# Gated linear attention with an MLP on one core: keys and queries of the first eight chunks interleaved in pairs of heads and transposed as 32-bit words

## The chip, the cores and the metric

The kernel runs on one core of one Trainium2 chip. The metric is the device time of one execution in microseconds (us). The kernel before took 193.82 us, the median of three runs (193.76 to 194.22). A trace of one execution comes from the hardware profiler. Its engines are PE (TensorE matmul), PEld (its weight loads), DVE (VectorE), ACT (ScalarE), POOL (GpSimd) and SP (SyncE, which issues most DMAs). "L588" is line 588 of the kernel before.

## What is computed

Inputs are q, k, v, a_re and a_im of shape (4, 8, 768, 48) in float32: 4 batches, 8 heads, 768 steps, 48 channels. The first half is a linear recurrence with complex decay, of which only the real part is read out:

```
scale = min(|a|, 0.999) / (|a| + 1e-6)          # per head, step and channel
S_re, S_im = a_re*S_re - a_im*S_im + k (x) v,  a_re*S_im + a_im*S_re     # a scaled
y[t] = q[t] @ S_re
```

The heads of y are put side by side (384 channels). The second half is a layer norm and a two-layer MLP with ReLU of width 1536, added to its input; the result is (4, 768, 384) in float32.

## The kernel before, in words

The 768 steps of a batch are six chunks of 128. Two chunks make a pair; there are twelve pairs P (three to a batch) and 24 chunks n = 2P + c. All chunk tiles have the 128 steps on the partitions.

For each pair the logarithm of the decay is summed along the steps by matmuls with a triangle (`dec`, L472), and so is its phase (`ph`, L487 to L493). ACT makes `en` = exp(-sum) and `e` = exp(sum) (L476) and the two trigonometric factors `trig` (sine L509, cosine L520 or L532). `ke` = k * en and `qe` = q * e (L539 to L547, a product of a 32-bit and a 16-bit tile) are then multiplied by cosine (a = 0) and sine (a = 1) into `ks` and `qs` (L548 to L558). These two have 128 columns for each head: 48 of cosine, 16 zeros, 48 of sine, 16 zeros. The zeros are written once for each of the three buffers of a ring (`pad`, L353 to L356). Pair 0 is made in two halves of four heads each (`PARTS`, L31), so its products have half the size and twice the number; the other pairs make all eight heads in one instruction, and `ke` and `qe` chunk by chunk.

For each chunk `ks` and `qs` are transposed: in chunks 0 to 7 on TensorE, one 128x128 block of bf16 for each head into one PSUM bank (`f_tr`, L585 to L588, groups `kT` and `qT`), then copied as one 128x1024 bf16 tile to `ksT` and `qsT` by DVE or ACT (`f_cp`, L590 to L598). Many later chunks use a transposing DMA instead (L593). With the transposed tiles, per head:

```
am = ksT.T @ qsT        # L611, 128 columns; masked by DVE into atm
G  = ks.T @ v           # L639, 48 columns: the state that goes to the next chunk
y  = atm.T @ v + qsT.T @ G      # L661 and L664, 48 columns
```

`y` becomes `x`; statistics (L674), a transpose (L682), two matmul stages (`mm1` L715, `relu` L726 or L728, `mm2` L736) and a last step (`ot`) finish the chunk. `dps` (L568) reads the last row of `e` for the decay of the state.

The order of all work is a list written out in the file (`PLAN`, L39 to L141): each entry names an operation, its engine and its PSUM bank, and each engine executes its own entries in that order. "op:G@other" makes the first instruction of a POOL operation wait for the last of another one. Buffers come from rings (L25); an operation waits until the former readers of its buffer are done. The matmuls `warm.0` to `warm.60` in the start have no reader.

The entries around the start that the change touches are, shortened to their engines: on DVE the six products of pair 0, `qs.0.0.1 ks.0.0.1 ks.0.1.0 qs.0.1.1 ks.0.1.1 ks.0.0.0`, then `decc.1 qs.0.1.0 qs.0.0.0 ksT.1 qsT.0 decc.0 qs.1.0.1 qs.1.0.0`; on PE `kT.1 kT.0 qT.0 qT.1`; on ACT `qsT.1`, then `ksT.0`; on POOL `qe.1.0.1` behind `qs.0.0.0`, `ke.1.0.1` behind `qs.1.0.0`, then `ke.1.0.0` and `v.0`, for which `gm.0` on PE (L639) waits.

Of the kernel before, what the change touches and what calls it, by code (L numbers as in the profile page):

```python
# [43 lines left out]
warm.18:P0 pick:G warm.19:P0 iv.0.1:A r.0.0:V warm.20:P0 q.1.0:S iv.1.0:A warm.21:P0 warm.22:P0 r2.0.0:V
warm.23:P0 r.0.1:V warm.24:P0 u.0.0:A warm.25:P0 q.0.1:S warm.26:P0 r2.0.1:V warm.27:P0 uth:V u.0.1:A
warm.28:P0 r.1.0:V warm.29:P0 gln:S warm.30:P0 warm.31:P0 warm.32:P0 r2.1.0:V warm.33:P0 warm.34:P0 are.2.0:S
warm.35:P0 warm.36:P0 l.0.0:V warm.37:P0 warm.38:P0 tab.trig.1:A th.0.1:A warm.39:P1 lc.0.0:V th.1.0:A
ph.0.1:P0 k.0.0:S dec.0.0:P1 th.0.0:A car.0.1:V0 l.0.1:V sin.0.1:A0 q.0.0:S ph.0.0:P2 warm.40:P3 warm.41:P3
# [5 lines left out]
tab.trig.3:A sin.0.0:A2 ke.0.1.0:V cos.0.1:A0 qt.0.0:P2 lc.2.0:V sin.1.0:A4 warm.59:P3 qs.0.0.1:V warm.60:P3
ks.0.0.1:V cos.0.0:A2 ks.0.1.0:V qt.1.0:P4 qs.0.1.1:V th.2.0:A ks.0.1.1:V dps.1:P0 ks.0.0.0:V cos.1.0:A4
kT.1:P2 decc.1:V0 qs.0.1.0:V kT.0:P0 qs.0.0.0:V ksT.1:V2 qT.0:P3 qe.1.0.1:G@qs.0.0.0 qT.1:P4 qsT.0:V3 mask:G
aim.3.0:S tab.log.4:A en.1.0:A6 wp.0:P5 decc.0:V1 qs.1.0.1:V qsT.1:A4 dec.2.0:P2 qs.1.0.0:V vf.1.1:S wc.0.0:V5
ke.1.0.1:G@qs.1.0.0 ksT.0:A0 am.1:P6 wc.0.1:V5 qT.3:P4 vf.1.0:S ke.1.0.0:G e.2.0:A2 wc.0.2:V5 am.0:P0
en.2.0:A2 v.0:G q.2.1:S qsT.3:V4 ks.1.0.0:V ln.3.0:A gm.0:P2 q.2.0:S ph.2.0:P4 atm.1:V6 ks.1.0.1:G@ks.1.0.0
G.0:A2 iv.3.0:A k.2.0:S gm.1:P2 qT.2:P3 atm.0:V0 y.1:P6 r.3.0:G k.2.1:S kT.3:P7 G.1:V2 wp.1:P0 qsT.2:V3  # L60
tab.trig.5:A sin.2.0:A4 are.4.0:S y.0:P1 kT.2:P2 ksT.3:V7 x.0:A1 v.1:G qt.2.0:P4 th.3.0:A ksT.2:V2 xtr.0:P7
aim.4.0:S wl.1:G gm.2:P1 wc.1.0:V0 x.1:A6 ph.3.0:P2 G.2:A1 wc.1.1:V0 qe.2.0.0:G cos.2.0:A4 xtr.1:P6 wc.1.2:V0
gm.3:P1 xT.0:A7 qe.2.0.1:G am.3:P4 sin.3.0:A2 xT.1:V6 wp.2:P0 atm.3:V4 qs.2.0.0:G car.3.0:A2 am.2:P6 qt.3.0:P2
# [11 lines left out]
ot.1:V2 mm2.3.1:P1 iv.6.0:A bn.2:V mm1.2.0.1:P4 st.0:S bn.4:V rstd.1:G mm1.2.0.0:P4 st.1:S qs.3.0.1:V
mm1.2.1.1:P6 qs.3.0.0:V tab.trig.7:A th.5.0:A mm2.3.2:P1 ks.3.0.1:V relu.2.0:A4 ot.2:V0 mm1.2.1.0:P6 l.5.0:V
st.2:S qT.6:P2 th.4.0:A vf.3.1:S qT.7:P0 q.4.0:S qe.4.0.1:G@l.5.0 qsT.6:A2 kT.7:P3 qsT.7:V0 are.8.0:S
ph.4.0:P4 ke.4.0.0:G ksT.7:V3 relu.2.1:A6 are.7.0:S ot.3:V1 kT.6:P0 sin.4.0:A4 mm1.2.2.0:P2 r.6.0:V abs.4.0:A4
am.7:P6 vf.4.1:S ksT.6:V0 ke.4.0.1:G@r.6.0 mm1.2.2.1:P2 car.4.0:A4 atm.7:V6 cos.4.0:A am.6:P0 k.5.0:S
qe.4.0.0:G mm2.5.0:P4 v.3:A atm.6:V0 ph.5.0:P6 q.6.0:S relu.2.2:A2 lc.5.0:V gm.6:P5 q.5.1:S mm2.5.1:P4  # L80
ks.4.0.0:V abs.5.0:A6 G.6:V5 y.6:P0 mm2.4.0:P1 sin.5.0:A6 k.5.1:S r2.6.0:V ks.4.0.1:V dps.3:P2 cos.5.0:A
aim.7.0:S y.7:P3 x.6:V0 qs.4.0.0:G@ks.4.0.1 mm2.4.1:P1 th.6.0:A x.7:V3 xtr.6:P0 bn.7:V xtr.7:P3 decc.3:A2
aim.8.0:S mm2.4.2:P1 xT.6:A0 bn.5:V gm.7:P5 dec.5.0:P6 qs.4.0.1:V rstd.2:G kT.8:P0 G.7:V5 qsT.8:S tab.log.8:A
en.5.0:A6 mm2.5.2:P4 xT.7:V3 v.4:G ksT.8:V0 mm1.3.1.1:P2 e.5.0:A6 ot.5:V4 k.6.0:S ke.5.0.0:G mm1.3.1.0:P2
u.6.0:A st.3:S mm1.3.0.1:P6 relu.3.1:A2 l.6.0:V vf.6.0:S gm.8:P0 mm1.3.0.0:P6 G.8:A0 qe.5.0.1:V q.5.0:S
ln.8.0:A mm1.3.2.0:P4 ot.4:V1 lc.6.0:V mm1.3.2.1:P4 q.7.0:S iv.8.0:A relu.3.0:V6 ke.5.0.1:G@lc.6.0 gm.9:P0
kT.9:P1 relu.3.2:A4 dps.4:P2 bn.6:V ks.5.0.1:G dec.6.0:P6 ln.7.0:A ksT.9:V1 qT.9:P3 ks.5.0.0:V iv.7.0:A
am.8:P4 mm2.6.0:P1 qsT.9:V3 decc.4:A2 ksT.10:S r.7.0:G@ks.5.0.0 en.6.0:A6 mm2.6.1:P1 G.9:V0 e.6.0:A6 atm.8:V4
mm2.7.0:P0 vf.6.1:S am.9:P2 vf.5.1:S qe.5.0.0:G r2.7.0:A mm2.7.1:P0 st.4:S atm.9:V2 st.5:S qe.6.0.0:G y.8:P4
u.7.0:A k.6.1:S kT.11:P5 x.8:V4 y.9:P2 r.8.0:G vf.5.0:S ph.6.0:P6 x.9:V2 bn.8:V q.6.1:S xtr.9:P4 xtr.8:P2  # L90
tab.trig.9:A sin.6.0:A6 mm2.7.2:P0 xT.9:V4 qs.5.0.1:G xT.8:V2 abs.6.0:A6 ksT.11:V5 mm2.6.2:P1 bn.9:V
mm1.4.0.1:P2 cos.6.0:A rstd.3:G qs.5.0.0:V mm1.4.2.1:P4 car.6.0:A6 l.7.0:V qsT.10:S mm1.4.2.0:P4 th.7.0:A
ke.6.0.1:V mm1.4.0.0:P2 v.6:A ot.7:V0 are.9.0:S ke.6.0.0:G@ke.6.0.1 mm1.4.1.0:P6 relu.4.0:A2 relu.4.2:V4
aim.9.0:S mm1.4.1.1:P6 v.5:A q.7.1:S qT.11:P2 lc.7.0:V relu.4.1:V6 ph.7.0:P4 qe.6.0.1:G@lc.7.0 qsT.11:A2
k.7.1:S dps.6:P0 ks.6.0.1:G ot.6:V1 car.7.0:A4 am.10:P6 k.7.0:S decc.6:A0 r2.8.0:A gm.10:P1 atm.10:V6
mm2.8.0:P0 th.8.0:A qs.6.0.0:G mm2.8.1:P0 abs.7.0:V4 sin.7.0:A4 am.11:P2 mm2.9.0:P6 ks.6.0.0:V rstd.4:G
G.10:V1 dec.7.0:P4 ksT.13:S atm.11:V2 qs.6.0.1:G mm2.8.2:P0 tab.log.10:A u.8.0:A y.10:P1 q.8.1:S ot.8:V0
kT.12:P7 st.7:S x.10:A1 l.8.0:V y.11:P2 ln.9.0:A qsT.12:S qT.13:P3 x.11:V2 mm2.9.1:P6 e.7.0:A4 qsT.13:V3
k.8.0:S xtr.11:P0 en.7.0:A4 xtr.10:P1 qe.7.0.0:G mm2.9.2:P6 are.10.0:S xT.10:V1 xT.11:V0 iv.9.0:A am.13:P2
# [702 lines left out]
```

## Time and profile before

| | |
|---|---|
| runs | 194.22, 193.82, 193.76 us; median 193.82 |
| span of the profiled execution | 193.1 us (its own time outside the span is not given) |
| mean granted TensorE clock | 0.986 |
| busy shares | PE 91%, PEld 69%, DVE 79%, ACT 83%, POOL 54% |
| chain that ended last | PE 52%, DVE 17%, ACT 12%, DMA 7% |
| transposes of ks and qs on PE (L588) | 200 in all, 128 of them in chunks 0 to 7; 5% of the chain |
| DMA | 37.04 MB, 192 GB/s in the mean |

The span is the time from the first to the last instruction. "Busy" is the time in which an engine has an instruction in work; matmuls overlap, so the duration of one (219 ns for a transpose) is longer than the distance to the next. The chain is followed back from the last instruction, at each step to what released it or to the instruction before it on its engine; its pieces are what the time is made of. A stretch or a slice gives the same busy times for a part of the span. The granted clock is the share of full speed that TensorE was given.

### The profile page before, as it was taken

The numbers are of one execution on the slowest core, as the hardware profiler recorded it, in microseconds if no ns is written. First come the engines' busy times: TensorE is split into PE (matmuls) and PEld (weight loads), VectorE is DVE, ScalarE is ACT, GpSimd is POOL, SyncE is SP. The second block draws the span as 40 slices with busy tenths as digits, with TensorE's granted clock in tenths as the row PEclk, the third lists the DMA queues.
The fourth block names the chain that finished last, engine by engine and source line by source line (L and its number), as shares of the span: only waits on it lengthen the run. The fifth ranks groups of instructions, "written<-read, shape, count | busy, mean of one in ns | idle before, by whom it ended". The sixth has DMA issues, their size and how long they took to land.

```text
span 193.1 us, 5126 instructions
## 1 busy us (share of the span) xinstructions
PE 175.3 (91%) x2042; PEld 133.6 (69%) x2042; DVE 151.7 (79%) x276; ACT 159.4 (83%) x222; POOL 104.8 (54%) x123
## 2 busy tenths in 40 slices
PE   5856597999999999999999989999989897999991
PEld 3643386689876877877867856868658676776860
DVE  0578979999779999799988978997987695657422
ACT  3899989979999999999989898888999856463460
POOL 8403038998334435489595950544857715593110
PEclk9999969999999999999999999999999999999998
DMA  5999999999999699979999997999997999997132
GB/s 159 275 215 185 201 207 239 213 188 220 210 201 214 195 260 231 220 152 226 188 233 168 212 220 106 195 235 205 230 196 150 140 203 147 252 127 203 44 122 83
DMA packets 129992, 37.04 MB, mean 192 GB/s; under 512 B 124976, under 2 KB 129584, under 8 KB 129968
## 3 DMA queue, kind: packets, MB, share of 16 engines
q1 hardware_dynamic: 128016, 34.35, 85.7%
q0 software_dynamic: 1952, 2.36, 7.4%
q8 instruction: 16, 0.26, 0.6%
q14 instruction: 8, 0.07, 0.1%
HBM read 28.31 MB, written 4.72 MB: 171 GB/s over the span
## 4 chain that ended last, share of the span: by engine, by line
PE 52%; DVE 17%; ACT 12%; DMA 7%; SPq 4%; issue 4%; POOL 2%; DVEq 0%; ACTq 0%
PE banks L736 16%; PE banks L715 15%; PE banks L588 5%; PE banks L611 3%; DMA qsT<-qs 3%; DMA aim<-in_a_im_dram 2%; SPq L593 2%; PE banks L491 2%; ACT L770 2%; DVE l L461 2%; DMA k<-in_k_dram 2%; ACT trig L509 2%; ACT th L480 2%; PE banks L661 2%; PE banks L682 2%
## 5 line engine op out<-in xcount | busy, mean ns | idle before, releaser
L736 PE MATMUL banks<-w2b,h 128*128 128x384 bf16 x288 | 54.5, 326 | 0.7 <-ACT trig L509 0.6
L715 PE MATMUL banks<-xT,w1b 128*128 128x256 bf16 x432 | 51.3, 273 | 0.0
L715 PEld LDWEIGHTS <-w1b 128*128 128x128 bf16 x432 | 41.3, 98 | 6.3 <-DVE xT L286 0.4
L736 PEld LDWEIGHTS <-h 128*128 128x128 bf16 x288 | 26.1, 97 | 14.6 <-issue 1.1
L289 DVE TENSOR_TENSOR atm<-banks,mask 128x1024 bf16<-128x1024 f32 x24 | 28.9, 1219 | 7.4 <-PE banks L611 7.2
L726 ACT ACTIVATE h<-banks 128x1024 bf16<-128x1024 f32 x26 | 26.3, 1020 | 5.4 <-PE banks L715 5.2
L289 POOL TENSOR_TENSOR qe<-q,e 128x384 bf16<-128x384 f32 x18 | 16.4, 917 | 22.8 <-DVE qs L289 8.4
L289 POOL TENSOR_TENSOR qs<-qe,trig 128x768 bf16<-128x768 bf16 x12 | 19.6, 1641 | 7.7 <-DVE ks L289 5.5
L770 ACT ACT_TABLE_LOAD x17 | 21.8, 1283 | 1.1 <-PEq L786 0.8
L289 POOL TENSOR_TENSOR ke<-k,en 128x384 bf16<-128x384 f32 x16 | 14.5, 916 | 9.9 <-DVE l L464 5.6
L289 POOL TENSOR_TENSOR ks<-ke,trig 128x768 bf16<-128x768 bf16 x9 | 14.7, 1642 | 7.7 <-DVE ks L289 6.8
L611 PE MATMUL banks<-qsT,ksT 128*128 128x128 bf16 x192 | 14.6, 219 | 1.7 <-DMA qsT<-qs 1.7
L728 DVE TENSOR_SCALAR h<-banks 128x1024 bf16<-128x1024 f32 x10 | 12.1, 1214 | 4.9 <-PE banks L715 4.9
L748 POOL TENSOR_TENSOR ot<-ot,x 128x384 f32<-128x384 f32 x8 | 7.2, 914 | 15.8 <-ACT ot L741 15.8
L611 PEld LDWEIGHTS <-ksT 128*128 128x128 bf16 x192 | 12.0, 97 | 4.0 <-issue 2.6
L491 PE MATMUL banks<-th,u_th 128*128 128x384 f16 (+1 forms) x52 | 11.9, 313 | 2.5 <-ACT th L480 2.5
L750 DVE SCALAR_TENSOR_TENSOR ot<-banks,rstd,x 128x384 f32<-128x384 f32 x16 | 9.8, 612 | 5.4 <-PE banks L736 3.5
L461 DVE SCALAR_TENSOR_TENSOR l<-r,w 128x768 f16<-128x768 f16 (+1 forms) x13 | 12.0, 926 | 2.0 <-ACT r L457 1.8
L674 DVE BATCH_NORM_STATS2 stats<-x 128x6 f32<-128x384 bf16 x24 | 13.1, 546 | 0.0
L289 POOL TENSOR_TENSOR r<-aim,are 128x768 f16<-128x768 f32 x6 | 10.9, 1817 | 4.1 <-ACT are L445 4.1
L443 ACT ACTIVATE w<-are 128x768 f32<-128x768 f32 (+1 forms) x13 | 10.3, 797 | 2.5 <-DMA are<-in_a_re_dram 2.5
L457 ACT ACTIVATE r<-r,one_b 128x768 f16<-128x768 f16 (+1 forms) x13 | 11.5, 887 | 0.7 <-DVE r L289 0.6
(95 smaller groups left out, 372.6 us busy)
## 6 DMA issues: line engine op xcount, KB each, us to landing
k<-in_k_dram SPq DMA_DIRECT2D x24, 192.0 KB, 4.1
q<-in_q_dram SPq DMA_DIRECT2D x24, 192.0 KB, 4.1
vf<-in_v_dram SPq DMA_DIRECT2D x24, 192.0 KB, 4.1
out_dram<-ot SPq DMA_DIRECT2D x24, 192.0 KB, 3.1
are<-in_a_re_dram SPq DMA_DIRECT2D x11, 384.0 KB, 4.5
aim<-in_a_im_dram SPq DMA_DIRECT2D x11, 384.0 KB, 4.9
w1b<-in_moe_w_ch_dram POOLq DMA_DIRECT2D x1, 1152.0 KB, 11.1
w2b<-in_moe_w_ch_dram POOLq DMA_DIRECT2D x1, 1152.0 KB, 12.5
```

What stands on the lines that cost most here:

```text
L289: {"DVE": nc.vector, "POOL": nc.gpsimd}[eng(name)].tensor_tensor(**kw)
L443: add(f"ln.{X}", lambda S_=S_: act(out=S_("w"), in_=S_("are"), func=AF.Ln), needs=[f"are.{X}"], uses=[("are", P), ("w", P)])
L457: add(f"u.{X}", lambda S_=S_: act(out=S_("r2"), in_=S_("r2"), func=AF.Ln, bias=one_b), needs=[f"r2.{X}", "one"], uses=[("r2", P)])
L461: nc.vector.scalar_tensor_tensor(out=S_("l"), in0=S_("r2"), scalar=0.5, in1=S_("w"), op0=ALU.mult, op1=ALU.add)
L491: nc.tensor.matmul(heads(ps[:, c]), lhsT=u_th[:, c, j], rhs=step(T("th", P), j), start=False, stop=(j == R - 1), skip_group_check=True)
L611: nc.tensor.matmul(ps[:, h], lhsT=T("ksT", n)[:, h], rhs=T("qsT", n)[:, h], start=True, stop=True)
L674: nc.vector.bn_stats(out=T("stats", n), in_=T("x", n))
L715: nc.tensor.matmul(ps[:, jj], lhsT=w1b[:, dc, ts(gi * JG + jj, C)], rhs=T("xT", P)[:, dc].rearrange("p c t -> p (c t)"), start=(dc == 0), ...
L726: act(out=dst, in_=src, func=AF.Relu)
L728: nc.vector.tensor_scalar(out=dst, in0=src, scalar1=0.0, scalar2=None, op0=ALU.max)
L736: nc.tensor.matmul(bank(f"o.{n}")[:, 0:DM], lhsT=T("h", P)[:, j, ts(c, C)], rhs=w2b[:, j], start=(j == 0), stop=(j == NJ - 1))
L770: g.add(f"tab.{nm}.{i}", lambda tab=tab: nc.scalar.preload_act_table_set(tab))
```

## The change

In pairs 0 to 3 (chunks 0 to 7) the tiles `e`, `en`, `trig`, `ke`, `qe`, `ks` and `qs` hold heads h and h + 4 interleaved, element by element, so that two bf16 values of the two heads are one 32-bit word. A chunk of `ks` is then four blocks of 128 words: 48 words of cosine, 16 zero words, 48 of sine, 16 zero words. `f_tr` transposes four blocks of 32-bit words with a second identity in float32; the bank has as many bytes as before, and the copies out of it are the same. The matmuls that read `ks`, `ksT` or `qsT` of these chunks take every second element. The zeros lie elsewhere than in the plain layout: the early pads are as many and as large as before but placed for the new layout, and pairs 4, 5 and 6, the first plain users of each buffer, get pads of their own. In the plan, `ident4` follows `ident`, and six pads on POOL are added; no other entry is moved.

```diff
+PAIRED = {0, 1, 2, 3}
...
+    ident4 = pool.tile([C, C], FP32, name="ident4")
...
+    g.add("ident4", lambda: make_identity(nc, ident4), needs=["ue"])
...
+        paired = P in PAIRED
+        def plain(ap):
+            return ap.rearrange("p c (b x) -> p c b x", b=2) if paired and NS == 1 else ap
+        def woven(ap, i):
+            if not paired:
+                return ap[:, :, ts(i, W)]
+            ap = ap.rearrange("p c (x b) -> p c b x", b=2)
+            return ap if NS == 1 else ap[:, :, i]
+        def lane(ap, h):
+            if not paired:
+                return ap[:, h]
+            return ap.rearrange("p (i x) t -> p i (x t)", x=2).rearrange(
+                "p i (t b) -> p i t b", b=2)[:, h % 4, :, h // 4]
...
-                    out=T(nm, P)[:, :, fs], in_=view(f"dec.{X}"), func=AF.Exp, scale=sc),
+                    out=woven(T(nm, P), i), in_=plain(view(f"dec.{X}")), func=AF.Exp, scale=sc),
...
-                out=T("trig", P)[:, 1, :, fs], in_=v16(), func=AF.Sin, scale=TWO_PI_SAFE / TURN),
+                out=woven(T("trig", P)[:, 1], i), in_=plain(v16()), func=AF.Sin,
...
+                        tt(f"{nm}.{X}.{m}", out=woven(T(nm, P)[:, cs], i),
+                           in0=plain(T(src, P)[:, cs, hs].rearrange("p c h d -> p c (h d)")),
+                           in1=woven(T(dc_, P)[:, cs], i), op=ALU.mult)
...
+                        if paired:
+                            views = [T(nm, P).rearrange("p c (i x) f -> p (c i) (x f)", x=2)[
+                                :, :, ds(a * C, 2 * D)]] + [
+                                ap.rearrange("p c (i e) -> p (c i) e", e=2 * D)
+                                for ap in (T(src, P), T("trig", P)[:, a])]
+                            if NS > 1:
+                                views = [ap.rearrange("p n (d b) -> p n d b", b=2)[:, :, :, i]
+                                         for ap in views]
+                            tt(f"{nm}.{X}.{a}", out=views[0], in0=views[1], in1=views[2], op=ALU.mult)
...
+                    if paired:
+                        nc.gpsimd.memset(t.rearrange("p (n x) -> p n x", x=C)[:, :, 2 * D:C], 0.0)
+                    elif fresh:
+                        nc.gpsimd.memset(t.rearrange("p (n x) -> p n x", x=HALF)[:, :, D:HALF], 0.0)
+                    else:
+                        nc.gpsimd.memset(t.rearrange("p (n x) -> p n x", x=C)[:, :, D:HALF], 0.0)
...
             def f_tr(nm, o, c):
+                if paired:
+                    both = T(nm, P)[:, c].rearrange("p h f -> p (h f)").bitcast(FP32)
+                    for i in range(H // 2):
+                        nc.tensor.transpose(bank(o)[:, ts(i, C)], both[:, ts(i, C)], ident4)
+                    return
...
-                    nc.tensor.matmul(ps[:, h], lhsT=T("ksT", n)[:, h], rhs=T("qsT", n)[:, h],
+                    nc.tensor.matmul(ps[:, h], lhsT=lane(T("ksT", n), h), rhs=lane(T("qsT", n), h),
...
-                        nc.tensor.matmul(heads(ps)[:, h], lhsT=T("ks", P)[:, c, h],
+                        nc.tensor.matmul(heads(ps)[:, h], lhsT=lane(T("ks", P)[:, c], h),
...
-                        nc.tensor.matmul(ps[:, h], lhsT=T("qsT", n)[:, h], rhs=T("G", n - 1)[:, h],
+                        nc.tensor.matmul(ps[:, h], lhsT=lane(T("qsT", n), h), rhs=T("G", n - 1)[:, h],
```

In the plan (additions in the order of their places):

```diff
 ident:G
+ident4:G
...
+pad.ks.4:G
 ks.4.0.0:V
...
+pad.qs.4:G
 qs.4.0.0:G@ks.4.0.1
...
+pad.ks.5:G
 ks.5.0.1:G
...
+pad.qs.5:G
 qs.5.0.1:G
...
+pad.ks.6:G
 ks.6.0.1:G
...
+pad.qs.6:G
 qs.6.0.0:G
```

More of the change, by code (lines that the diff above doesn't have):

```diff
@@ L44 @@
[L44 to L48, printed above, removed]
@@ L54 @@
[L54 to L58, printed above, removed]
@@ L59 @@
[L59 to L63, printed above, removed]
@@ new lines @@
+warm.51:P3 warm.52:P3 warm.53:P3 warm.54:P3 warm.55:P3 warm.56:P3 qe.0.1.0:V warm.57:P3 warm.58:P3 tab.trig.3:A
+sin.0.0:A2 ke.0.1.0:V cos.0.1:A0 qt.0.0:P2 lc.2.0:V sin.1.0:A4 warm.59:P3 qs.0.0.1:V warm.60:P3 ks.0.0.1:V cos.0.0:A2
+ks.0.1.0:V qt.1.0:P4 qs.0.1.1:V th.2.0:A ks.0.1.1:V dps.1:P0 ks.0.0.0:V cos.1.0:A4 kT.1:P2 decc.1:V0 qs.0.1.0:V
+kT.0:P0 qs.0.0.0:V ksT.1:V2 qT.0:P3 qe.1.0.1:G@qs.0.0.0 qT.1:P4 qsT.0:V3 mask:G aim.3.0:S tab.log.4:A en.1.0:A6
+wp.0:P5 decc.0:V1 qs.1.0.1:V qsT.1:A4 dec.2.0:P2 qs.1.0.0:V vf.1.1:S wc.0.0:V5 ke.1.0.1:G@qs.1.0.0 ksT.0:A0 am.1:P6
@@ new lines @@
+wc.0.1:V5 qT.3:P4 vf.1.0:S ke.1.0.0:G e.2.0:A2 wc.0.2:V5 am.0:P0 en.2.0:A2 v.0:G q.2.1:S qsT.3:V4 ks.1.0.0:V ln.3.0:A
+gm.0:P2 q.2.0:S ph.2.0:P4 atm.1:V6 ks.1.0.1:G@ks.1.0.0 G.0:A2 iv.3.0:A k.2.0:S gm.1:P2 qT.2:P3 atm.0:V0 y.1:P6 r.3.0:G
+k.2.1:S kT.3:P7 G.1:V2 wp.1:P0 qsT.2:V3 tab.trig.5:A sin.2.0:A4 are.4.0:S y.0:P1 kT.2:P2 ksT.3:V7 x.0:A1 v.1:G
+qt.2.0:P4 th.3.0:A ksT.2:V2 xtr.0:P7 aim.4.0:S wl.1:G gm.2:P1 wc.1.0:V0 x.1:A6 ph.3.0:P2 G.2:A1 wc.1.1:V0 qe.2.0.0:G
+cos.2.0:A4 xtr.1:P6 wc.1.2:V0 gm.3:P1 xT.0:A7 qe.2.0.1:G am.3:P4 sin.3.0:A2 xT.1:V6 wp.2:P0 atm.3:V4 qs.2.0.0:G
@@ L75 @@
[L75 to L99, printed above, removed]
@@ new lines @@
+mm2.7.0:P0 vf.6.1:S am.9:P2 vf.5.1:S qe.5.0.0:G r2.7.0:A mm2.7.1:P0 st.4:S atm.9:V2 st.5:S qe.6.0.0:G y.8:P4 u.7.0:A
+k.6.1:S kT.11:P5 x.8:V4 y.9:P2 r.8.0:G vf.5.0:S ph.6.0:P6 x.9:V2 bn.8:V q.6.1:S xtr.9:P4 xtr.8:P2 tab.trig.9:A
+sin.6.0:A6 mm2.7.2:P0 xT.9:V4 pad.qs.5:G qs.5.0.1:G xT.8:V2 abs.6.0:A6 ksT.11:V5 mm2.6.2:P1 bn.9:V mm1.4.0.1:P2
+cos.6.0:A rstd.3:G qs.5.0.0:V mm1.4.2.1:P4 car.6.0:A6 l.7.0:V qsT.10:S mm1.4.2.0:P4 th.7.0:A ke.6.0.1:V mm1.4.0.0:P2
+v.6:A ot.7:V0 are.9.0:S ke.6.0.0:G@ke.6.0.1 mm1.4.1.0:P6 relu.4.0:A2 relu.4.2:V4 aim.9.0:S mm1.4.1.1:P6 v.5:A q.7.1:S
@@ new lines @@
+qT.11:P2 lc.7.0:V relu.4.1:V6 ph.7.0:P4 qe.6.0.1:G@lc.7.0 qsT.11:A2 k.7.1:S dps.6:P0 pad.ks.6:G ks.6.0.1:G ot.6:V1
+car.7.0:A4 am.10:P6 k.7.0:S decc.6:A0 r2.8.0:A gm.10:P1 atm.10:V6 mm2.8.0:P0 th.8.0:A pad.qs.6:G qs.6.0.0:G mm2.8.1:P0
+abs.7.0:V4 sin.7.0:A4 am.11:P2 mm2.9.0:P6 ks.6.0.0:V rstd.4:G G.10:V1 dec.7.0:P4 ksT.13:S atm.11:V2 qs.6.0.1:G
+mm2.8.2:P0 tab.log.10:A u.8.0:A y.10:P1 q.8.1:S ot.8:V0 kT.12:P7 st.7:S x.10:A1 l.8.0:V y.11:P2 ln.9.0:A qsT.12:S
+qT.13:P3 x.11:V2 mm2.9.1:P6 e.7.0:A4 qsT.13:V3 k.8.0:S xtr.11:P0 en.7.0:A4 xtr.10:P1 qe.7.0.0:G mm2.9.2:P6 are.10.0:S
@@ new lines @@
+r2.11.0:A k.10.0:S bn.15:V mm2.14.0:P4 relu.7.1:A0 ke.9.0.0:G relu.7.2:V2 mm2.13.2:P6 vf.9.1:S rstd.7:G gm.16:P5
+am.17:P0 ks.9.0.1:V q.10.1:S mm2.14.1:P4 ot.13:V6 qe.9.0.0:G@ks.9.0.1 tab.trig.13:A th.10.0:A atm.17:V0 mm2.14.2:P4
+q.10.0:S dps.9:P2 cos.9.0:A am.16:P6 st.12:S decc.9:V2 ph.10.0:P0 G.16:A5 k.10.1:S atm.16:V6 ks.9.0.0:G th.11.0:A
+mm2.15.0:P5 sin.10.0:A0 car.10.0:V0 y.16:P2 qe.9.0.1:V ksT.19:S y.17:P3 x.16:V2 dec.10.0:P6 qs.9.0.0:G@qe.9.0.1
+x.17:V3 xtr.16:P2 mm2.15.1:P5 tab.log.14:A u.11.0:A xT.16:V2 xtr.17:P2 qs.9.0.1:G mm2.15.2:P5 en.10.0:A6 xT.17:V2
@@ new lines @@
+bn.16:V mm1.8.0.1:P2 abs.10.0:A0 l.11.0:V mm1.8.0.0:P2 e.10.0:A6 qsT.19:S mm1.8.1.1:P0 oa.14:A4 lc.11.0:V mm1.8.2.1:P6
+oa.15:A5 relu.8.0:V2 v.9:G@lc.11.0 ksT.18:S mm1.8.1.0:P0 ke.10.0.0:G mm1.8.2.0:P6 qsT.18:S ke.10.0.1:G ph.11.0:P4
+tab.trig.15:A cos.10.0:A relu.8.2:V6 relu.8.1:A0 dps.10:P2 k.11.0:S ks.10.0.1:V gm.18:P3 k.11.1:S am.19:P6 G.18:A3
+vf.10.1:S qe.10.0.0:G@ks.10.0.1 mm2.16.0:P0 sin.11.0:A4 atm.19:V6 mm2.16.1:P0 ks.10.0.0:G abs.11.0:A4 gm.19:P3
+am.18:P6 cos.11.0:A G.19:V3 mm2.17.0:P1 atm.18:V6 qe.10.0.1:G ksT.20:S mm2.17.1:P1 y.19:P3 qs.10.0.0:V y.18:P6
```

169 lines of the change are left out of this document (92 added, 77 removed).

## The prediction

> **What bounds the kernel now.** I read the busy table and the 40 slices first, then the busy time of each engine by stretches, then the chain of work that ended last, then the groups of instructions by line with shapes kept apart, and last the timelines of DVE and POOL around the places that the diff touches.
>
> The page gives the whole: PE is busy for 91% of the span, and from the eighth slice to the last nearly without a hole (third line: tenths of each slice).
>
> ```profile
> PE 175.3 (91%) x2042; PEld 133.6 (69%) x2042; DVE 151.7 (79%) x276; ACT 159.4 (83%) x222; POOL 104.8 (54%) x123
> ...
> PE   5856597999999999999999989999989897999991
> ```
>
> The stretches (columns: the stretch, its length, then busy us of PE, PEld, DVE, ACT, POOL with instruction counts, the granted clock, the DMA share, GB/s) show how the first third runs. All 128 transposes of the first eight chunks lie between 23.8 and 77 us.
>
> ```profile
> 23.80:27.30 3.50, 3.48 (x33) 3.40 (x34) 2.47 (x8) 2.74 (x3) 1.35 (x3) 0.53 0.91 180
> ...
> 51.00:60.00 9.00, 9.00 (x101) 6.06 (x99) 7.38 (x12) 8.85 (x14) 3.85 (x5) 1.00 0.95 205
> 60.00:68.00 8.00, 8.00 (x83) 6.52 (x82) 7.49 (x17) 7.97 (x11) 4.24 (x6) 1.00 0.84 209
> 68.00:77.00 9.00, 9.00 (x126) 6.58 (x125) 8.78 (x18) 8.87 (x14) 4.17 (x5) 1.00 1.10 248
> ```
>
> Three things are to be seen. The first 32 transposes ran at a granted clock of 0.53. From 51 to 77 us PE has no idle time, but ACT has only 0.31 us (26 less 8.85, 7.97 and 8.87): a faster PE soon waits for ACT there. From 35 to 44 us (not shown) the same holds for DVE, busy for 8.95 of 9.00 with PE at 9.00.
>
> The chain (start, length, what) tells which of them sets the time. In the start it runs through DVE, then the first transposes, then one link through ACT and POOL, and from 31.24 to 77 us through PE alone.
>
> ```profile
> 22.41 0.54 DVE ks L289 x2
> 22.95 0.27 DVE qs L289
> 23.22 0.55 DVE ks L289 x2
> 23.77 0.05 issue
> 23.82 3.47 PE banks L588 x32
> 27.31 1.02 ACT qsT L284
> ...
> 31.24 0.36 PE banks L639 x8
> ...
> 32.77 0.45 PE banks L588 x8
> ```
>
> So a transposed 16-bit block costs 3.47 / 32 = 108 ns at the start and 0.45 / 8 = 56 ns later. The mean durations of 219 to 236 ns in the groups are latencies; the chain has the spacing, and that is what I use.
>
> **The change, part by part.**
>
> Transposes. The eight chunks have 16 groups (kT and qT) of 8 blocks; they become 16 groups of 4 blocks of 32-bit words: 64 in place of 128. Sixteen of them lie in the slow start, 48 in the warm stretch. No row shows a 32-bit matmul. From below, a block could cost what one 16-bit block costs: 56 ns warm, 108 cold, and then 48 x 56 = 2.7 us of PE go away. From above, four times that (224 and 432 ns), if the array takes the word in several passes; then 48 x 112 = 5.4 us are added. I take 112 ns (217 cold): the block holds twice the bytes of the row next to it, and at the same bytes per ns it costs what the two blocks that it replaces cost. Then PE gains nothing in the warm stretch.
> The Trainium skill ("TensorE: Matmul & The Clock Gate", section "Terms") names a transpose mode that is four times faster for FP32; an estimate by it would be the lower bound here, and 48 x 56 = 2.7 us would be saved on PE. No row of this trace bears on it; it is the first rival.
>
> Strided operands. The heads lie interleaved, so 64 products of keys and queries (L611) read both operands at every second element, and 56 of L639 and 48 of L664 read their weights so (so do 48 small ones of L568, which end before their readers need them). Their rows, with two of DVE for the part after:
>
> ```profile
> L611 PE MATMUL banks<-qsT,ksT 128*128 128x128 bf16 x192 | 14.6, 219 | 1.7 <-DMA qsT<-qs 1.7
> ...
> L639 PE MATMUL banks<-v,ks 128*128 128x48 bf16 x160 | 7.2, 183 | 1.4 <-POOL v L409 1.2 <-DVE G L286 0.2
> ...
> L289 DVE TENSOR_TENSOR qe<-q,e 128x384 bf16<-128x384 f32 x6 | 3.3, 549 | 0.0
> ...
> L289 DVE TENSOR_TENSOR qs<-qe,trig 128x384 bf16<-128x384 bf16 x4 | 1.3, 354 | 0.0
> ```
>
> In the chain L639 and L664 stand 25 ns apart (0.20 us for 8 of them at 36.25, and 0.05 for each pair of L661 and L664), L611 56 ns apart (0.45 for 8). The gain is bounded by zero, since the instructions and their sizes stay. The loss is bounded by 104 x 31 = 3.2 us, if a strided weight load takes the 56 ns of a whole block, and by 64 x 56 = 3.6 us more, if a strided stream runs at half rate. I take zero, because the moving operands of L491 and L472 already come in runs of 48 with gaps and keep 0.33 us for 2 x 384 columns, full rate; both ends stay in the range.
> The Trainium skill (the same page, section "Weight-path perf modes") says that fast weight loading works on packed or strided weights but not on FP32. An estimate by it leaves the strided loads free, as I have it; no run shows it.
>
> VectorE at the start. Pair 0 is made in two halves of the heads, so all eight products ks and qs of pair 0 read and write every second element. The two DVE rows above are the price: 16-bit packed operands take 354 ns, an operand that is not packed 16-bit takes 549 ns; in the timeline the instructions stand 0.27 us and 0.47 us apart. So +0.2 us each, 8 x 0.2 = 1.6 us, of which six instructions (1.2 us) lie ahead of the first transposes, and two more ahead of qT. All of it is on the chain (22.06 to 23.77). The products ke and qe have a 32-bit input and stay at 549 ns. Those of pairs 1 to 3 have whole runs of 96 elements and keep the rate; nothing on DVE changes there. The activations that make e, en, sin and cos now write every second element. They take 810 ns for 768 from 32-bit words and 815 from every second 16-bit half, so a gap in the source costs nothing; I put zero on a gap in the target too. If it halved the rate, as on DVE, it would be 16 x 0.8 = 13 us on ACT; nothing in the rows points there, since ACT already runs at about one element a ns.
>
> The start put together. kT.1 starts at 23.82 + 1.2 = 25.0. With 4 x 217 = 0.87 us a group, kT ends at 26.75, after the last qs (24.79 + 1.6 = 26.4), and qT ends at 28.5 where it ended at 27.29: +1.2 us. Behind qT.0 on DVE wait its copy (26.46), decc.0 and qs.1.0.0 (which ended at 28.46); POOL starts ke.1.0.1 behind that one by the order in the plan (28.59), then v.0, and PE waited 1.19 us for v.0 at 31.24. Each link starts when the one before it ends, so L639 at 31.24 moves by 1.2 us, and PE has no hole until 77 us in which this could be caught up.
>
> GpSimd. One identity in 32 bits is added after the 16-bit one (0.22 + 0.51 us at 15.7 to 16.5), ahead of a wait of 8.38 us for qs: covered. The early pads are six of 512 elements as before (0.53 us each). Six new pads of 256 elements cost some 0.3 us each (a memset of 128 takes 0.21, one of 512 0.53). Those of pair 4 stand in a wait of 3.26 us before 73.69. Those of pairs 5 and 6 stand in a full stretch of POOL (81.69 to 93, 95.90 to 103), which ends in idle times of 0.85 and 2.35 us: 0 to 0.6 us for what POOL makes there; I take zero. Nothing is queued on SP or on another DMA queue.
>
> **Sum.** +1.2 us at the start, 0 in the warm stretch, 0 on POOL: 193.82 + 1.2 = 195.0. The span is 193.1, and the runs are 193.76 to 194.22 with a median of 193.82, so 0.7 us lie around the span; the page does not give the profiled execution's own time apart from its span, so I put the sum on the median.
>
> **Rivals.**
>
> 1. Halved blocks, 0.30. A 32-bit block costs what a 16-bit one does. At the start the last qs (26.4) then holds qT, which ends at 27.27 as before, but DVE copies qT.0 at 27.1, not 26.46: L639 moves by 0.6 us. After that PE saves 2.7 us. For it: PE is full in this stretch. Against it: ACT has 0.31 us of idle time from 51 to 77 us, and DVE 0.05 from 35 to 44. Between all of it (0.6 - 2.7 = -2.1 us) and nothing (+0.6) comes through: 191.7 to 194.4, most likely 193.3. It decides from about 90 ns a block downwards, where 48 x 22 ns = 1.1 us outweigh the start.
> 2. Four passes, 0.20. Cold, the 16 blocks take 16 x 432 = 6.9 us from 25.0, ending at 31.9, +4.6 us; warm, 48 x 112 = 5.4 us on a PE without holes. Together 203.8; with a clock that rises sooner under the longer burst about 200. It decides from some 130 ns a block.
> 3. Strided operands cost, 0.14. Blocks even, but 3.2 us for the weights and up to 3.6 for the streams: 198.2 to 201.8, less if only part of the loads slow down. Against it: no gap in moving runs costs anything now.
>
> My forecast has 0.36 (194.4 to 195.8). It also holds when blocks are halved and strided weight loads eat it: 0.6 - 2.7 + 3.2 = +1.1.
>
> **How the numbers follow.** About 0.3% (0.6 us) is what a measurement of this kernel can tell from no change. Faster than 193.24 is a little over half of the first rival: 0.17. Within, 193.24 to 194.40, are the rest of it and a little of the forecast: 0.16. All else is slower: 0.67. The range leaves out most of the four passes and the far ends: 192.2 to 200.6.
>
> **What would show it.** Right: 64 blocks on the transposes' line, a group of four in 0.45 us in the chain (0.22 for the first rival, 0.9 for the second); the eight products of pair 0 at 549 ns; kT.1 at 25.0; L639 at 25 ns apart still, or near 56; the first L639 at 32.4. The forecast is wrong if kT.1 starts before 24.5, or if a warm group of four blocks is far from 0.45 us, or if PE shows new holes between 35 and 77 us behind ACT.

## The result, and the profile after

The changed kernel took 196.81 us, the median of four runs (195.82 to 198.28), beside 193.95 for the kernel before: 1.0146 times as long, 95% interval 1.0104 to 1.0187. On a second chip it was 196.88 beside 194.68, 1.0088 (1.0058 to 1.0119). So it is slower, by 1.7 to 2.9 us. The profiled execution took 198.28 us, the longest of the four, with a span of 196.2; 2.1 us lie around the span, and with the kernel before it is 1.7 in the median.

The page of the kernel after (busy time; tenths of each slice of PE; the granted clock by slices; the chain by engine):

```profile
PE 177.0 (90%) x1978; PEld 133.8 (68%) x1978; DVE 154.2 (79%) x276; ACT 162.4 (83%) x222; POOL 108.6 (55%) x131
...
PE   5767586999999999999999989999998999989991
...
PEclk9978859999999999999999999999999999999999
...
PE 38%; ACT 24%; DVE 19%; issue 7%; POOL 4%; DMA 4%; SPq 1%; DVEq 0%; ACTq 0%; POOLq 0%
```

PE issues 64 matmuls less and is busy for 1.7 us more. ACT has 3.0 us more work in the same 222 instructions, DVE 2.5 and POOL 3.8. ACT's share of the chain doubles (12% to 24%). The clock, which before dipped in one slice only, is low in four; its row before was

```profile
PEclk9999969999999999999999999999999999999998
```

The same stretches as before, moved by the 2.7 and 3.6 us by which the work is late there:

```profile
26.50:30.00 3.50, 3.50 (x18) 3.37 (x19) 2.64 (x7) 2.36 (x3) 1.44 (x3) 0.59 1.05 263
54.60:63.60 9.00, 9.00 (x99) 6.06 (x98) 7.32 (x11) 8.88 (x14) 3.83 (x5) 1.00 0.67 141
63.60:71.60 8.00, 7.96 (x66) 6.40 (x64) 7.41 (x17) 7.97 (x10) 4.37 (x6) 1.00 0.47 123
71.60:80.60 9.00, 9.00 (x127) 6.58 (x125) 8.77 (x18) 8.87 (x14) 4.68 (x7) 1.00 0.98 220
```

From 54.6 to 80.6 us PE is nearly as full as before (0.04 us idle) and ACT has 0.28 us of idle time in 26: nothing is caught up here. One new hole lies ahead of it: at 41.1 us `am` waits 0.18 us for ACT's cosine. Most of the loss lies at the start. The chain there:

```profile
23.43 0.58 DVE qs L286
24.01 0.94 DVE ks L286 x2
24.96 0.47 DVE qs L286
25.42 0.95 DVE ks L286 x2
26.50 3.35 PE banks L634 x16
29.88 1.02 ACT qsT L281
...
34.30 0.36 PE banks L690 x8
35.83 0.47 PE banks L634 x4
...
37.23 1.04 ACT trig L520
```

From the first of the six products to kT it is 3.07 us, where it was 1.76 (22.06 to 23.82). Sixteen 32-bit blocks take 3.35 us where 32 of 16 bits took 3.47, but here the clock was full again for the last 0.45 us. Where it was low throughout, in two runs that follow (after_again and p0_source), sixteen take 3.65 us and 32 of 16 bits 3.53:

```profile
25.11 3.65 PE banks L634 x16
...
24.55 3.53 PE banks L644 x32
```

The last link of the chain above is new: an activation of 1.04 us on the path. The groups (L634 is the 32-bit transpose, L662 `am`, L690 `G`, L532 and L520 cosine and sine):

```profile
L662 PE MATMUL banks<-qsT,ksT 128*128 128x128 bf16 x192 | 14.7, 219 | 0.4 <-DMA qsT<-qs 0.2 <-ACT trig L532 0.2
...
L690 PE MATMUL banks<-v,ks 128*128 128x48 bf16 x160 | 7.2, 183 | 2.0 <-POOL v L420 1.8 <-DVE G L283 0.2
...
L634 PE MATMUL banks<-ident,ks 128*128 128x128 f32 x32 | 5.6, 313 | 0.9 <-DVE ks L286 0.9
...
L532 ACT ACTIVATE trig<-banks 128x768 bf16<-128x768 int16 x3 | 3.2, 1057 | 0.5 <-PE banks L528 0.5
...
L286 DVE TENSOR_TENSOR qs<-qe,trig 128x384 bf16<-128x384 bf16 x4 | 2.2, 586 | 0.0
...
L599 POOL MEMSET qs<- 128x512 bf16 x3 | 1.6, 528 | 0.0
...
L532 ACT ACTIVATE trig<-banks 128x384 bf16<-128x384 int16 x2 | 1.2, 605 | 0.0
...
L603 POOL MEMSET qs<- 128x256 bf16 x3 | 0.9, 313 | 0.0
```

Here `am` and `G` keep 219 and 183 ns, and the products of pair 0 went from 354 to 586. The cosine of pairs 1 to 3, which writes every second element, went from 820 (three of 128x768) to 1057. Its rows before:

```profile
L520 ACT ACTIVATE trig<-banks 128x768 bf16<-128x768 int16 x3 | 2.5, 820 | 0.6 <-PE banks L516 0.6
...
L520 ACT ACTIVATE trig<-banks 128x384 bf16<-128x384 int16 x2 | 1.0, 496 | 0.0
```

ACT executes the same list in both kernels, so one number tells how late the whole work stands: the start of an ACT instruction less the start of the same one before. I took it from the timelines of ACT, in us, for the kernels that follow as well. The head is the time in the kernel before.

| kernel | 18.8 | 31.6 | 54.5 | 63.1 | 93.8 | 114.4 | 152.5 | 160.3 | 169.1 | 186.2 |
|---|---|---|---|---|---|---|---|---|---|---|
| after | 1.41 | 3.06 | 3.36 | 3.64 | 3.76 | 3.85 | 3.84 | 3.08 | 2.35 | 3.09 |
| after_again | 0.00 | 1.94 | 2.25 | 2.52 | 2.64 | 2.73 | 2.73 | 1.97 | 0.79 | 0.69 |
| tr16 | -0.18 | 1.34 | 1.67 | 1.94 | 2.08 | 2.39 | 2.40 | 2.37 | 2.15 | 1.95 |
| act_only | 0.22 | 1.31 | 1.61 | 1.85 | 1.84 | 1.99 | 1.99 | 1.86 | 1.70 | 1.51 |
| source_gap | -0.30 | 1.44 | 1.43 | 1.45 | 1.57 | 1.65 | 1.64 | 0.89 | -0.06 | 0.90 |
| p0_only | 0.35 | 1.82 | 1.92 | 1.92 | 1.90 | 1.90 | 1.87 | 1.12 | -0.14 | 1.74 |
| p0_source | 0.68 | 0.97 | 1.03 | 1.04 | 1.16 | 1.25 | 1.24 | 0.49 | -0.65 | -0.72 |
| tr32_again | 0.75 | 1.00 | 1.03 | 1.02 | 1.01 | 1.00 | 0.98 | 0.23 | -1.03 | -1.24 |

The lateness comes in steps and stands still between them, to some hundredths of a microsecond over up to 40 us. The changed kernel loses in the start, a little at 37 to 40 and 56 to 59, a little more at 87 and 109, and gets something back after 155, of which this execution loses a part again at 170 to 173.

### The profile page after: what moved, and what is told of

It reads as the page before. It is cut to its first block, busy times and chain, and to the rows that moved or that the text cites. A ratio compares the mean times of both kernels' runs of the same rounds, so it can differ in the third digit from the quotient of the medians.

```text
span 196.2 us, 5006 instructions
## 1 busy us (share of the span) xinstructions
PE 177.0 (90%) x1978; PEld 133.8 (68%) x1978; DVE 154.2 (79%) x276; ACT 162.4 (83%) x222; POOL 108.6 (55%) x131
## 4 chain that ended last, share of the span: by engine, by line
PE 38%; ACT 24%; DVE 19%; issue 7%; POOL 4%; DMA 4%; SPq 1%; DVEq 0%; ACTq 0%; POOLq 0%
PE banks L766 13%; PE banks L787 11%; ACT th L491 3%; ACT h L777 3%; PE banks L634 3%; ACT L821 3%; PE banks L662 2%; DMA aim<-in_a_im_dram 2%; PE banks L502 2%; ACT trig L520 2%; DVE atm L286 2%; DVE l L472 2%; ACT r L468 2%; ACT e L487 2%; POOL qs L286 2%
## 5 line engine op out<-in xcount | busy, mean ns | idle before, releaser
L787 PE MATMUL banks<-w2b,h 128*128 128x384 bf16 x288 | 54.5, 326 | 0.9 <-ACT trig L520 0.6
L286 POOL TENSOR_TENSOR qe<-q,e 128x384 bf16<-128x384 f32 x18 | 16.8, 941 | 24.1 <-DVE qs L286 10.2
L502 PE MATMUL banks<-th,u_th 128*128 128x384 f16 (+1 forms) x52 | 12.9, 336 | 3.1 <-ACT th L491 3.1
L662 PE MATMUL banks<-qsT,ksT 128*128 128x128 bf16 x192 | 14.7, 219 | 0.4 <-DMA qsT<-qs 0.2
L662 PEld LDWEIGHTS <-ksT 128*128 128x128 bf16 x192 | 12.1, 97 | 2.5 <-issue 0.7
L520 ACT ACTIVATE trig<-banks 128x768 bf16<-128x768 int16 (+1 forms) x13 | 10.8, 834 | 1.8 <-DVE sh L541 1.5
```

The lines of the kernel that those rows point to most:

```text
L286: {"DVE": nc.vector, "POOL": nc.gpsimd}[eng(name)].tensor_tensor(**kw)
L502: nc.tensor.matmul(heads(ps[:, c]), lhsT=u_th[:, c, j], rhs=step(T("th", P), j), start=False, stop=(j == R - 1), skip_group_check=True)
L520: add(f"sin.{X}", lambda i=i, v16=v16: act(out=woven(T("trig", P)[:, 1], i), in_=plain(v16()), func=AF.Sin, scale=TWO_PI_SAFE / TURN), nee ...
L662: nc.tensor.matmul(ps[:, h], lhsT=lane(T("ksT", n), h), rhs=lane(T("qsT", n), h), start=True, stop=True)
L787: nc.tensor.matmul(bank(f"o.{n}")[:, 0:DM], lhsT=T("h", P)[:, j, ts(c, C)], rhs=w2b[:, j], start=(j == 0), stop=(j == NJ - 1))
```

## The experiments

**The theory** is that three parts cost time: the eight products of pair 0, which lose the packed rate (as forecast); ACT's stores to every second element in pairs 1 to 3 (which I had put at nothing); and little else, the 32-bit blocks being even. **The rivals**: the lower granted clock of the start is all of it; the 32-bit transposes cost by themselves; the strided operands or the pads cost. Each expectation says what it stands for. The kernel before ran beside every group of kernels: 193.86 us in the first (tr32_alone, act_flat, p0_plain, tr16), 194.68 in the second (after_again, p0_only, act_only, both_flat), 194.01 in the third.

**Transposes alone.** The changed kernel with 16-bit transposes (tr16):

```diff
-                if paired:
+                if False:
```

> The changed kernel, but ks and qs of chunks 0 to 7 are transposed as eight 16-bit blocks; all else stays interleaved, so the products use wrong columns. Theory A: no change against the changed kernel, 196.8 us within 0.8. Rival B: the clock at the start is that of before and the time falls below 195.5 us.

Measured: 196.96 us, 1.0158 (1.012 to 1.0195), no faster than the changed kernel. Its chain, at a mean clock of 0.982, is the cleanest view of the start:

```profile
24.84 3.29 PE banks L638 x32
...
32.57 0.37 PE banks L690 x8
```

The first L690 is at 32.57, 1.33 us later than before, where I had forecast 1.2. The 32-bit transposes do not make the loss, nor does a low mean clock alone: two executions at 0.982 took 196.8 and 196.7 us, those of the kernel before beside them at 0.981 and 0.982 193.3 to 194.1.

The other way round, the kernel before with 32-bit transposes and nothing else (tr32_alone, repeated as tr32_again, and in chunks 2 to 7 only as tr32_warm, with `0 < P < 4`):

```diff
+                if P < 4:
+                    both = T(nm, P)[:, c].rearrange("p h f -> p (h f)").bitcast(FP32)
+                    for i in range(H // 2):
+                        nc.tensor.transpose(bank(o)[:, ts(i, C)], both[:, ts(i, C)], ident4)
+                    return
```

> The kernel before with one part of the change alone: in chunks 0 to 7 the plain ks and qs are transposed as four 32-bit blocks, with the second identity; nothing is interleaved, so the products that follow use wrong columns of the same sizes. Theory A (the 32-bit block costs what the two 16-bit blocks cost, 110 to 117 ns against 112, and the time lies in the strided stores of ACT and in pair 0): the time of before, 193.9 us, within 0.5 us. Rival B (the 32-bit transposes change how busy TensorE looks and cost it granted clock at the start): one or two more windows of low clock in the first 40 us and 195 us or more.

> A second look, on another chip, at the kernel before with 32-bit transposes in chunks 0 to 7 and nothing else changed (the heads are not interleaved, so the transposed values lie in the wrong places). Theory (blocks cost 110 to 117 ns for 2 x 56 before, so there is nothing to win): 1.000 +- 0.003. Rival (half the PE instructions, or fewer waits on them, give 0.6 us back, as the first run's 0.9965 said): 0.9965 +- 0.003 again.

> The same in chunks 2 to 7 alone: chunks 0 and 1, which are transposed at a low granted clock in the start, keep their 16-bit transposes (nothing is interleaved, so the values of chunks 2 to 7 lie in the wrong places). If 32-bit transposes win 0.6 us in the start (209 ns cold for 2 x 108), this run is at 1.000 +- 0.003 and the other at 0.9965; if they win in the warm stretch, both are at 0.9965; if they win nothing, both are at 1.000.

Measured: 193.29 us, 0.9965 (0.9931 to 0.9998); again 193.53, 0.9962 (0.9931 to 0.9994); chunks 2 to 7 only 193.22, 0.9936 (0.9909 to 0.9963). So 32-bit transposes give 0.7 us or somewhat more back, and the cold ones of the start have no part in it. My theory had nothing here. It does not come from PE's time for the blocks; what the traces say of it, which falls short of proof, is told below.

**ACT's stores.** The changed kernel with whole runs stored in pairs 1 to 3 (act_flat), and the kernel before with gapped stores there and no other change (act_only):

```diff
 act_flat
-                    out=woven(T(nm, P), i), in_=plain(view(f"dec.{X}")), func=AF.Exp, scale=sc),
+                    out=stored(T(nm, P), i), in_=source(view(f"dec.{X}")), func=AF.Exp, scale=sc),
 act_only
-                    out=T(nm, P)[:, :, fs], in_=view(f"dec.{X}"), func=AF.Exp, scale=sc),
+                    out=gapped(T(nm, P)[:, :, fs]), in_=halves(view(f"dec.{X}")), func=AF.Exp, scale=sc),
```

(sine and cosine likewise).

> The changed kernel, but in pairs 1 to 3 the activations that make e, en, sin and cos write their 768 elements without gaps; their readers still take every second element, so heads are mixed up. Theory A: these 12 activations fall from 1.04 to 1.07 us to 0.81, which is 12 x 0.25 = 3.0 us of ACT, on an engine that the chain of the changed kernel follows from 56 to 88 us; most of it comes through, 195.0 us (194.3 to 195.8), and the start stays as late as in the changed kernel. Rival B (the clock at the start makes the difference): 196.5 us, since the start is not touched.

> The kernel before, but in pairs 1 to 3 the activations that make e, en, sin and cos write every second element (the two halves of the heads interleaved); nothing else changes, so heads are mixed up in what follows. Theory A: 12 x 0.25 = 3.0 us more of ACT work, of which 1 to 2 us come through: 195.2 us (194.6 to 196.0). Rival C: with the start on time ACT's idle time between 27 and 51 us takes most of it, 194.2 us or less.

Measured: act_flat 195.68 us, 1.0078 (1.0049 to 1.0108); act_only 196.11, 1.0053 (1.0024 to 1.0082). The gapped stores alone make the kernel before slower, by 1.0 us (0.5 to 1.6).

If the gap costs only in the target, it can be moved: read from two halves of the source, write whole runs (source_gap; the values are those of the changed kernel):

```diff
+        def stored(ap, i):
+            return ap.rearrange("p c (x b) -> p c x b", b=2) if paired and NS == 1 else woven(ap, i)
+        def source(ap):
+            return ap.rearrange("p c (b x) -> p c x b", b=2) if paired and NS == 1 else plain(ap)
```

> The changed kernel whole, with one edit: in pairs 1 to 3 the activations that make en, e, sin and cos write whole runs and read every second element from two halves of their source, so the same interleaved values come about with the gap on the reading side. Theory (a gap in an activation's target costs 0.25 us for 128x768, a gap in its source nothing, as the 815 ns of the cosine from every second 16-bit half suggest): the means of these lines go back to 0.81 to 0.83 us, ACT is busy for about 160 us, and the time is that of the run whose stores were flat and whose values were not interleaved, 1.0078 +- 0.003 times the kernel before, instead of 1.009 to 1.015. Rival (the gap costs on whichever side it is): 1.03 to 1.07 us for each and the time of the changed kernel.

Measured: 195.33 us, 1.0086 (1.0057 to 1.0114), as act_flat. Its groups (L538 is the cosine, L493 en):

```profile
L493 ACT ACTIVATE en<-banks 128x768 bf16<-128x768 f32 x11 | 8.9, 807 | 0.1
...
L538 ACT ACTIVATE trig<-banks 128x768 bf16<-128x768 int16 x3 | 2.5, 825 | 0.6 <-PE banks L534 0.6
```

With the gap on the reading side the cosine is back at 825 ns, and ACT's busy time at 159.9 us. The times alone do not part it from the second run of the changed kernel (1.0088); the table does. From 31.6 to 63.1 the lateness grows by 0.58 us in after, 0.58 in after_again, 0.60 in tr16 and 0.54 in act_only, the four with gapped stores. It grows by 0.01 in source_gap and by 0.02 to 0.10 in the other three. The traces of three runs that are not in the table agree: 0.58 in p0_plain, which has the gapped stores, and 0.07 in act_flat and both_flat, which do not.

**Pair 0.** Pair 0 plain and pairs 1 to 3 interleaved (p0_plain), and the reverse (p0_only), with two pads added for pair 3, the first user of the other layout, and in p0_only those of pairs 4 to 6 left out:

```diff
 p0_plain
-PAIRED = {0, 1, 2, 3}
+PAIRED = {1, 2, 3}
 p0_only
-PAIRED = {0, 1, 2, 3}
+PAIRED = {0}
```

> The changed kernel with pair 0 left plain (PAIRED without 0): its products, activations and transposes are those of before, pairs 1 to 3 stay interleaved, and pair 3 gets two pads on POOL. Theory A: the start is that of before (first transposes at 23.8 us and not 26.5), which gives back some 1.2 to 1.6 us; ACT keeps its 3.0 us: 195.3 us (194.6 to 196.0). Rival B: granted clock at the start as before and 194.0 us.

> Pair 0 alone interleaved (PAIRED = {0}), pairs 1 to 3 plain and transposed in 16 bits; pair 3 gets two pads, pairs 4 to 6 none. Theory A: the start is later by 1.2 us and more, ACT gains only 8 x 0.1 us: 195.3 us (194.8 to 196.0), with the first matmul of L639 at 32.5 us or later where it was at 31.24. Rival C (the two parts cost only together, since a late start takes the slack that hides ACT's longer stores): 194.3 us.

Measured: p0_plain 194.80 us, 1.0039 (1.0013 to 1.0066); p0_only 195.66, 1.0029 (0.9997 to 1.006). Each part alone costs about half; p0_only by itself can hardly be told from no change. Between 18.8 and 31.6 its lateness grows by 1.47 us, and in tr32_again by 0.25. In its chain it is 3.09 us from the first product to kT, 1.33 more than before.

Pair 0 is not alone at the start. act_only grows by 1.09 us there and p0_plain by 0.52, both with pair 0 plain, and both_flat and p0_source by 0.29. Where pair 0 is plain, ACT's sine of pair 1 is a link of the chain ahead of the transposes. Here are p0_source and act_only:

```profile
22.59 0.71 ACT trig L526
...
22.16 0.93 ACT trig L515
```

So the gapped stores cost 0.22 us there as well; with pair 0 interleaved the products end later and hide it. The rest of act_only's 1.09 us goes with its clock, low for 10.2 us from 20.0 in this execution (3.4 in the profile of the kernel before).

**Both undone.** Pair 0 plain and flat stores (both_flat), and the version in which all is computed, with the gaps in the sources (p0_source). With them the changed kernel itself once more (after_again, no edit).

> The changed kernel with both suspected parts undone: pair 0 plain, and in pairs 1 to 3 the activations write without gaps (heads mixed up). Left over are the 48 32-bit transposes of the warm stretch, the matmuls with strided operands, the strided products ke and qe on DVE and POOL, and eight added pads. Theory A: the time of before, 193.9 us within 0.5. If the strided operands of TensorE or the pads cost something, 194.6 us or more.

> As the run with the gaps in the activations' sources, and with pair 0 left in the plain layout with 16-bit transposes; all of the computation is done. Theory (pair 0's eight products and the activations' gapped stores are all that the change costs): 0.998 +- 0.003 times the kernel before, as with flat stores. If the 32-bit transposes of themselves give something back, 0.7 us, it is not slower than that and may be below 0.997, which would be the version that beats both kernels. Rival (the pads, strided TensorE operands or a gapped source have a cost of their own): 1.003 or more.

> The changed kernel unaltered, for more executions of it: the first four spread over 195.8 to 198.3 us at granted clocks of 0.969 to 0.978, where 25 of the kernel before lie at 0.972 to 1.000, most at 0.98. Theory A (strided stores of ACT, and pair 0): 196.5 us, and at an equal clock of 0.98 still 195.5 or more. Rival B (a lower granted clock is all of it): executions at 0.98 take 194 us.

Measured: both_flat 194.24 us, 0.998 (0.995 to 1.0009); p0_source 193.71, 0.9972 (0.9945 to 0.9998); after_again 196.88, 1.0088 (1.0058 to 1.0119). With the two parts undone nothing is left of the loss, though 48 of the 64 32-bit blocks, the strided operands and eight pads are all still there. But these two runs also have what 32-bit transposes give back (0.9936 to 0.9965 alone). Beside those they are 0.1 to 0.4% longer: what is left of the change may cost some tenths of a microsecond, which the intervals do not part from none. p0_source beats both kernels, the one before by 0.3%, which its interval just parts from none and which is no more than the transposes gave alone. The one execution of after_again with a mean clock of 0.983 took 197.0 us, where the rival of the clock expected 194.

## Why the prediction was right, and where its sum was not

The time lies in the range, on the side that was forecast, 1.8 us above the predicted one. One of the signs that were to show the forecast wrong came true in small: a hole on PE behind ACT, of 0.18 us at 41.1 us. Step by step:

**32-bit blocks: right.** Groups of four stand at 0.47 to 0.49 us in the chain (forecast 0.45) and eight at 0.88, 110 to 122 ns a block; under the low clock it is 3.65 / 16 = 228 (217). Halved blocks and four passes are both out. An estimate by what the Trainium skill says of the transpose mode, four times faster for FP32 ("TensorE: Matmul & The Clock Gate", section "Terms"), would have given 56 ns; the trace does not agree.

**Strided operands: right.** In the chain eight L690 take 0.36 us at the start, where the same eight took 0.36 before; `am` and `G` keep their means; p0_source has the strided operands of six chunks and is no slower than before. The Trainium skill says that fast weight loads work on strided weights (the same page, "Weight-path perf modes"); the trace agrees.

**Pair 0 on DVE: right.** The products take 580 to 586 ns instead of 352 to 354. From the first to kT it is 1.31 us more (forecast 1.2). The products of pairs 2 and 3 keep their rate, as forecast (548 to 559 ns for `ks`). The Trainium skill ("VectorE: DVE Perf Modes", section "Mode 2×_1P — pack two bf16 into one 32-bit read") asks for 16-bit operands at a step of one; the trace agrees.

**ACT's stores: the step that was mis-sized.** I "put zero on a gap in the target too". It is 0.24 us for 128x768 (820 to 1057 ns) and 0.1 for 128x384 (496 to 605): twelve of one and eight of the other make 12 x 0.24 + 8 x 0.1 = 3.7 us by these rows, and the busy time, in which neighbours overlap, grew by 3.0. The whole rows of e, en and sine (810 to 874 ns over eleven, three of them gapped) say the same: 3 x 0.23 / 11 = 0.064. Some 0.55 us of it lies on the path, in the two places of the table between 31.6 and 63.1 (and 0.22 at the start where pair 0 is plain). I had seen that ACT has 0.31 us of idle time in 26 and looked only at what a faster PE would win by it, not at what a slower ACT would lose. The Trainium skill gives one rate for all activations ("ScalarE: Activation LUTs", section "Step-by-step: what each stage is for"). For stores with a gap the runs do not agree: they show 0.31 ns an element more.

**The pads: a little.** I had put those of pairs 5 and 6 at zero in 0 to 0.6. The table has +0.12 to 0.14 at 87 us in the kernels that have these pads (after, after_again, tr16, source_gap, p0_source) and 0.08 to 0.09 at 109 in all of these but tr16, and nothing in p0_only and tr32_again: 0.2 us. The traces show the way of the first step. The pad makes POOL's `ks` product start later, so that DVE's `ks` product beside it overlaps with it for 535 to 546 ns instead of 404 to 410. It then takes 952 to 959 ns instead of 819 to 824, and by the plan POOL's `r`, for which ACT waits, comes behind it. No run takes the pads out alone. (Between 93.8 and 114.4 us act_only has 0.15 and tr16 0.31, at 100 us; that step is not explained.)

**The granted clock: not in the sum.** In the profiled execution 1.41 us are lost before the first interleaved product (18.8 us), where the clock is low in slices three and four; the rest of the start is 1.31 for the products and 0.38 behind them. So the first L690 came at 34.30 and not at 32.4. Ten of the twelve executions of the changed kernel have 0.975 or less in the mean, of those before that the comparisons use 17 of 86. Executions of the kernel before with such a clock took 195.0, 195.1 and 194.9 us in the three groups, the others 193.8, 194.5 and 193.9: about 1.0 us. The difference in share, 0.64, makes some 0.6 us of the loss. That the longer wait on DVE brings the low clock about is not shown: of the executions of the changed kernel and the experiments, 33 of 50 with pair 0 interleaved have it and 33 of 84 without (act_only 7 of 12). The Trainium skill says of the clock gate that its window of 3.4 us runs free, so that one kernel has another number of slow matmuls from run to run ("TensorE: Matmul & The Clock Gate", "Part 1: The HAM clock gate"). The traces agree: before, the clock is low for 3.4 us from 24.0; after, for 3.4 from 12.3 and for 6.8 from 22.6.

**The tail: not in the sum either.** After 155 us every kernel of the table with 32-bit transposes wins 0.75 us at one place and 0.7 to 1.3 at the next, p0_only with two chunks of them too; tr16 and act_only, with none, win 0.0 to 0.2. The transposes had ended 75 us earlier. Not all of it is kept in every profile: at 170 to 180 us after loses 0.74 again, source_gap 0.96 and p0_only 1.88. There PE waits 0.79 and 1.01 us for ACT's `ot` in the first two, and 1.49 for a transposing DMA in p0_only. What waits there is `am`, for a transposing DMA of qs. The timeline of PE before:

```profile
152.00 0.61 PE L611 MATMUL banks<-qsT,ksT 128*128 128x128 bf16 x8 [0.59 <-DMA qsT<-qs]
...
163.88 0.61 PE L611 MATMUL banks<-qsT,ksT 128*128 128x128 bf16 x8 [1.11 <-DMA qsT<-qs]
```

The issue of these two on SP took twice as long as others (before, then after):

```profile
149.58 2.42 SPq L593 DMA_TRANSPOSE qsT<-qs  x1
...
160.72 2.59 SPq L593 DMA_TRANSPOSE qsT<-qs  x1
```

```profile
153.43 1.28 SPq L643 DMA_TRANSPOSE qsT<-qs  x1
...
164.70 1.57 SPq L643 DMA_TRANSPOSE qsT<-qs  x1
```

After, `am` waits for neither in the first place and 0.21 us in the second. In the kernel before the queue that brings instructions had a transfer in just these two stretches, 149 to 149.5 and 160 to 161 us (packets, MB, share):

```profile
q8 instruction: 1, 0.02, 18.6%
...
q8 instruction: 1, 0.02, 8.4%
```

After, these transfers lie at 147 to 148 and 158 to 159, and there the issues of other tiles take 2.17 and 2.28 us, with PE waiting for none. The profile lists 16 of them before and 15 after. In act_only and tr16 the transfer falls on the same two issues as before (2.26 and 2.62, 2.38 and 2.57 us), in p0_only and tr32_again it does not (1.29 and 1.59, 1.29 and 1.50). So the reading is: fewer PE instructions, instruction transfers at other moments, and by luck no longer on the two transposing DMAs that PE waits for. It rests on coincidence, not on an experiment that moves a transfer alone, which wasn't tried. In the fourteen traces 54 of 322 issues of a transposing DMA take 2.1 us or more; a transfer overlaps 40 of these 54 (not those of tr32_again at 77.71 and 121.14 us), but also 37 of the 268 shorter ones. So a transfer goes with a long issue often, and neither always nor alone.

The parts together: 1.2 to 1.3 for pair 0, 0.55 for the stores, 0.2 for the pads, 0.6 for the clock, less 0.7 for the tail by the times of the tr32 kernels, make 1.9 us. Measured were 2.8 and 1.7 by the ratios (2.9 and 2.2 by the medians), with intervals of about 0.8 and 0.6 on either side. The forecast had the first of these parts alone. That it missed by no more is in part luck, since the tail took back 0.7 that nobody had counted on. The lone profile of the kernel before has the tail's waits at their full size; how often its other executions have them stays open.

## What to carry to other kernels

Price a layout on each engine that writes or reads it: here the transposes and the matmuls took it for next to nothing, and DVE and ACT paid, since they had to make the gaps. If values must be interleaved, put the gap on the reading side of an activation, and leave plain what stands on the path of the start. And an engine with little idle time is a bound for losses, too: of the 0.5 us that two gapped stores add to ACT at 56 us, some 0.25 stay in the time, and of the 0.9 us of the four from 34 to 40 us some 0.3.

## What was not expected of the hardware

- An activation that stores every second 16-bit element takes 1057 ns for 128x768, against 820 with whole runs and 825 with the gap in the source.
- A 128x128 transpose of 32-bit words stands at 110 to 122 ns from the next one, and at 228 where the granted clock is 0.5: about the same per byte as 16-bit blocks at 56 and 110.
- A DVE product of 128x768 16-bit elements (`ks`) takes 548 ns, and 819 to 824 or 952 to 970 where it overlaps with POOL's `ks` or `qs` product for 404 to 410 or 535 to 558 ns.
- An issue of a transposing DMA on SP takes 1.2 to 1.9 us mostly, and 2.1 to 3.7 in 54 of 322 cases; an instruction transfer overlaps 40 of these 54 and 37 of the others.
- The mean granted clock of one kernel's executions lies between 0.969 and 1.0; those up to 0.975 take some 1.0 us longer.
- With 32-bit transposes 1.9 to 2.0 us lie outside the span (medians of ten runs; p0_only and tr16 have 1.8), and 1.7 before and in act_only.
